# One-core transformer block: four-bank exponentials, gelu straight from PSUM, more tiles turned by transfers, and a new timetable

## The chip, the cores and the metric

The kernel runs on one core of a Trainium2 chip. The metric is the device time of one execution in microseconds (us); smaller is better. The engines are named as in the profile: PE (TensorE, matmuls), PEld (its weight loads), DVE (VectorE), ACT (ScalarE), POOL (GpSimd) and SP (SyncE, which here only issues transfers). PSUM, into which PE writes, has eight banks of 512 fp32 columns.

## What is computed

A pre-layernorm transformer block on x of 2048 rows and 576 columns. The attention has 32 heads of 18 columns and works in four segments of 512 rows: causal softmax attention inside a segment, mixed by a learned gate with a linear-attention memory of the segments before. Then a feed-forward net (FFN) of 4608 columns with gelu. Both have a residual sum.

```python
for s in range(N):                      # N = 4 segments
    logits = einsum('bhqd,bhkd->bhqk', qs, ks) * scale + mask
    a_dot = einsum('bhqk,bhkd->bhqd', softmax(logits), vs)
    pq = phi(qs)                        # phi(t) = t + 1 if t > 0 else exp(t)
    a_mem = einsum('bhld,bhde->bhle', pq, M) / (einsum('bhld,bhd->bhl', pq, z)[..., None] + 1e-06)
    outs.append(g * a_mem + (1.0 - g) * a_dot)
    M = M + einsum('bhld,bhle->bhde', phi(ks), vs)
    z = z + einsum('bhld->bhd', phi(ks))
h = x + concat(outs) @ wo               # q, k, v from layernorm(x)
out = h + gelu(layernorm(h) @ w1 + b1) @ w2 + b2
```

## The kernel before

**Stages.** For each segment s: X (load x, layernorm, turn the tile so that columns lie on partitions), P (projections to q, k, v), A (attention), M (update of the memory), B (output projection, residual sum `h`, second layernorm, turning of the normalised tile into `x2T`), C (first FFN matmul F1, bias and gelu into `hT`), D (second FFN matmul F2, residual sum, output). A tile is 128 rows; a segment has four. In segment 0, stage C runs in two halves: C00 takes tiles 0 and 1, C01 tiles 2 and 3.

**What sets the order.** Each operation is added to a graph with the engines that it may run on. The table `TIMETABLE` (line 26), written into the file, gives each operation a rank and an engine (letter p, a, d, g or s); `Graph.schedule` (line 435) sorts all operations by rank, which fixes the order on every engine, and picks PSUM banks and buffers as it goes. So all engines run fixed sequences, and a late result holds up all that stands behind its reader on the same engine. All transfers but one go down SP's queue in that order; an issue that has to wait for data holds up the issues behind it.

**Tilings of PE.** A matmul uses the full array (128 rows), or half of the rows (two matmuls side by side), a quarter of the rows (scores of 32-row heads, lines 1094 and 1254), or a quarter of the columns (attention values and memory, lines 1125, 1279 and 1228). A projection has two forms, chosen by the order: if its two operations P and R stand side by side they are fused, mostly with full-height matmuls (line 906, with two of half height at an end, line 876); otherwise P and R run as half-height matmuls (line 876, 10 and 8 of them), the halves of the rows change PSUM banks between them, and R waits for a small memset (the mark, line 882) on DVE or POOL.

**Turning tiles.** There are two ways. `transposes` (line 823) uses PE: five (or four) transposes against the identity into a PSUM bank (line 829), then a copy by DVE or ACT into SBUF (lines 710, 706). `flip` (line 696) issues a transposing transfer from SP. In stage X, the pairs of tiles listed in `PE_X` (line 1504) use PE: all of segment 0 and tiles 0 and 1 of segment 1. In stage B of segment 0, tiles 0 and 1 use PE (two calls for each, since the FFN reads the columns in two shifted arrangements, columns 0 to 639 and 64 to 575), and tiles 2 and 3, listed in `DMA_FLIP_0`, use two transfers each.

**Exponentials.** A step of attention writes scores for four heads into two pairs of banks. `exp_of` (line 1045) reads each pair with an ACT instruction of its own (line 1048, 1024 columns), into half of the tile `pt`.

**FFN activation.** For segments 0 to 2, bias is added while a bank is moved from PSUM to `hT` on ACT (lines 1404, 1437) or DVE (lines 1406, 1439); later a few large ACT instructions run gelu in place over a batch of such tiles (lines 1411, 1445), since changing between exp and gelu loads an ACT table. In segment 3, gelu is taken straight from PSUM (line 1396).

**Residual sum in stage B.** The output projection lies in two banks; two DVE instructions of 288 columns add x (line 1331). Then come the statistics (lines 784, 785), the root on POOL (lines 799, 800), normalising (line 815) and a repeat of 64 columns (tail, line 1336).

## Time and profile before

| | |
|---|---|
| median of 3 runs | 440.61 us (440.54 to 441.11) |
| the profiled execution | 440.71 us |
| its span, first to last instruction | 439.0 us |
| granted TensorE clock | 1.000 |
| scores, exp, masks: ACT exponentials (line 1048) | 160, 1022 ns mean |
| first FFN matmuls (lines 1391, 1428) | 972 and 648 |
| second FFN matmuls (line 1480) | 1188 |
| DMA traffic | 72.05 MB, mean 164 GB/s |

The span in 40 slices of 11 us, busy tenths for each engine:

```profile
PE   8989999999999999999999999999999999999997
DVE  6999999988888777887988867585865102000021
ACT  6997978999798798768799977754596002646000
POOL 6888664647546574632522543234222010011010
DMA  7898489899889933965476638406244660650020
```

How to read a profile here: "busy" is the time in which an engine runs instructions; a row `L906 PE MATMUL bank<-hT,xreg ... x242 | 33.3, 287` is line 906, what it writes and reads, how often, total busy us and mean ns of one; what follows the second bar is idle time of the engine just before these, and what ended it. A matmul's own duration (287 ns) overlaps its neighbours, so the time that one occupies is read from the starts of neighbours or from a long group. `SPq` is SP's queue of issues; "landing" is the time from issue until the data is there. The tile names `hT`, `w_lo` and `xreg` are shared: the projection weights lie in `hT`'s space, and `xreg` holds both the turned x tiles and `x2T`.

### The profile page before, as it was taken

To read this page: it belongs to the slowest core of one execution; us is meant where nothing else is said; L and a number is where in the kernel's file an instruction comes from. 1 tells how busy PE (TensorE), PEld (TensorE's weight loads), DVE (VectorE), ACT (ScalarE), POOL (GpSimd) and SP (SyncE) were. 2 spreads that over 40 slices of the span, in tenths; PEclk is the share of its full clock that TensorE was granted. 3 is DMA by queue.
4 is the path that set the end of the run, shared out by engine and by line. 5 is a ranking of instruction groups with operands and counts; after the bars stand their busy time and mean duration, and the time that the engine had idled before them with its cause. 6 is when DMAs were issued, how large, how long until landed. Compare 5 with 4: busy or idle time off the path is not lost.

```text
span 439.0 us, 12146 instructions
## 1 busy us (share of the span) xinstructions
PE 431.3 (98%) x5080; PEld 276.8 (63%) x5080; DVE 285.9 (65%) x622; ACT 298.3 (68%) x328; POOL 175.6 (40%) x332
## 2 busy tenths in 40 slices
PE   8989999999999999999999999999999999999997
PEld 4766677775576676664445766644557775446776
DVE  6999999988888777887988867585865102000021
ACT  6997978999798798768799977754596002646000
POOL 6888664647546574632522543234222010011010
DMA  7898489899889933965476638406244660650020
GB/s 229 192 258 261 138 247 262 198 243 240 187 254 311 327 96 130 194 131 149 159 209 189 136 96 191 119 0 203 83 135 156 165 186 16 198 168 0 1 89 20
DMA packets 78422, 72.05 MB, mean 164 GB/s; under 512 B 57888, under 2 KB 65824, under 8 KB 78368
## 3 DMA queue, kind: packets, MB, share of 16 engines
q1 hardware_dynamic: 78224, 71.20, 59.5%
q8 instruction: 39, 0.64, 0.6%
q14 instruction: 15, 0.12, 0.1%
q10 hardware_dynamic: 144, 0.09, 0.1%
HBM read 42.30 MB, written 15.34 MB: 131 GB/s over the span
## 4 chain that ended last, share of the span: by engine, by line
PE 88%; DVE 7%; DMA 3%; issue 1%; SPq 1%; ACT 0%; DVEq 0%
PE bank L1480 33%; PE bank L1391 24%; PE bank L876 7%; PE bank L1428 7%; PE bank L906 6%; PE bank L1254 4%; PE bank L1279 3%; DMA w1g<-in_B_w_dram 2%; DMA hT<-in_A_w_dram 1%; PE bank L923 1%; DVE qk_pad L710 1%; PE bank L1094 1%; PE bank L1225 1%; DVE pt L1266 1%; PE bank L1125 1%
## 5 line engine op out<-in xcount | busy, mean ns | idle before, releaser
L1048 ACT ACTIVATE pt<-bank 128x1024 bf16<-128x1024 f32 x160 | 155.0, 1022 | 37.2 <-PE bank L1254 21.0
L1480 PEld LDWEIGHTS <-hT 128*128 128x128 bf16 x1188 | 111.7, 98 | 33.0 <-issue 5.8
L1391 PE MATMUL bank<-xreg,w1g 64*128 64x512 bf16 x972 | 108.3, 376 | 0.0
L1391 PEld LDWEIGHTS <-w1g 64*128 64x128 bf16 x972 | 46.6, 94 | 56.4 <-issue 3.4
L1480 PE MATMUL bank<-w,hT 128*128 128x288 bf16 (+2 forms) x594 | 77.5, 283 | 0.0
L1480 PE MATMUL bank<-w_lo,hT 128*128 128x288 bf16 (+2 forms) x594 | 77.2, 283 | 0.0
L1493 DVE TENSOR_TENSOR ot<-bank,hc 128x288 bf16<-128x288 f32 (+2 forms) x33 | 14.1, 443 | 91.7 <-PE bank L1480 90.0
L1268 POOL TENSOR_SCALAR_AFFINE_SELECT pt<-pt 128x512 bf16<-128x512 bf16 x56 | 38.3, 695 | 50.5 <-ACT pt L1048 48.4
L1396 ACT ACTIVATE hT<-bank,b_col 128x512 bf16<-128x512 f32 x36 | 22.3, 689 | 46.1 <-PE bank L1391 46.0
L1466 POOL TENSOR_TENSOR hc<-hc,b_bc 128x576 f32<-128x576 f32 x8 | 10.2, 1274 | 84.0 <-DMA hc<-hd 83.5
L1406 DVE TENSOR_SCALAR hT<-bank,b_col 128x512 bf16<-128x512 f32 x44 | 31.9, 739 | 17.0 <-PE bank L1391 16.0
L1428 PE MATMUL bank<-xreg,w1g 64*128 64x256 bf16 x648 | 38.5, 269 | 0.5 <-DVE qk_pad L710 0.3
L1428 PEld LDWEIGHTS <-w1g 64*128 64x128 bf16 x648 | 31.4, 94 | 6.7 <-issue 3.4
L906 PE MATMUL bank<-hT,xreg 128*128 128x288 bf16 x242 | 33.3, 287 | 0.0
L1411 ACT ACTIVATE hT<-hT 128x8192 bf16<-128x8192 bf16 (+2 forms) x6 | 31.8, 5321 | 0.4 <-DVE hT L1406 0.4
L906 PEld LDWEIGHTS <-xreg 128*128 128x128 bf16 x242 | 22.3, 98 | 7.4 <-issue 0.6
L1266 DVE TENSOR_TENSOR pt<-pt,tri 128x512 bf16<-128x512 bf16 x40 | 21.6, 557 | 8.1 <-ACT pt L1048 8.1
L876 PE MATMUL bank<-hT,xreg 64*128 64x288 bf16 x310 | 25.4, 285 | 1.2 <-DVE mark_dve L882 1.0
L1404 ACT ACTIVATE hT<-bank,b_col 128x512 bf16<-128x512 f32 x28 | 17.8, 686 | 12.3 <-PE bank L1391 11.9
L1439 DVE TENSOR_TENSOR hT<-bank,b_col 128x512 bf16<-128x512 f32 x33 | 21.7, 681 | 4.7 <-PE bank L1428 4.5
L1254 PE MATMUL bank<-qk 32*128 32x512 bf16 (+3 forms) x384 | 23.8, 301 | 0.0
L876 PEld LDWEIGHTS <-xreg 64*128 64x128 bf16 x310 | 14.5, 94 | 11.1 <-issue 5.9
(123 smaller groups left out, 564.0 us busy)
## 6 DMA issues: line engine op xcount, KB each, us to landing
w1g<-in_B_w_dram SPq DMA_DIRECT2D x41, 576.0 KB, 4.6
qkd<-qk_pad SPq DMA_DIRECT2D x12, 512.0 KB, 4.4
hd<-h SPq DMA_DIRECT2D x16, 288.0 KB, 2.7
hc<-hd SPq DMA_DIRECT2D x16, 288.0 KB, 3.7
w_lo<-in_B_w_dram SPq DMA_DIRECT2D x3, 864.0 KB, 5.4
w<-in_B_w_dram SPq DMA_DIRECT2D x3, 864.0 KB, 9.1
xb<-in_A_x_dram SPq DMA_DIRECT2D x16, 144.0 KB, 4.1
out_dram<-ot SPq DMA_DIRECT2D x15, 144.0 KB, 2.2
```

The costliest lines, as they stand in the source:

```text
L876: return nc.tensor.matmul(out=half(hf), lhsT=xTb.t[r, k, ts], rhs=wt[r, hf, k, :], start=start, stop=stop, skip_group_check=True)
L906: nc.tensor.matmul(out=half(hf), lhsT=xTb.t[:, k, ts], rhs=wt[:, hf, k, :], start=(k == 0 and b.form != "first"), stop=(k == n - 1 and b.f ...
L1048: ops.append(add(prio, {"act": 1.04}, lambda e, j=j: nc.scalar.activation(out=pt.t[:, 2 * j:2 * j + 2, :], in_=st[j].t[:], func=ACT.Exp, s ...
L1254: nc.tensor.matmul(out=st[i // 2].t[:, i % 2, off:off + n_], lhsT=qk[rows, 1, kt * P:(kt + 1) * P], rhs=qk[rows, 0, kt * P:L], start=True, ...
L1266: nc.vector.tensor_tensor(out=blk, in0=blk, in1=tri[:].unsqueeze(1).to_broadcast([P, 4, P]), op=ALU.mult)
L1268: nc.gpsimd.affine_select(out=blk, in_=blk, pattern=[[0, 4], [1, P]], compare_op=ALU.is_ge, fill=0.0, base=0, channel_multiplier=-1)
L1391: nc.tensor.matmul(out=cc[w].t[:], lhsT=w1.t[rows, k, q, :], rhs=x2T[s].t[rows, k, :], start=(k == 0), stop=(k == ND - 1))
L1396: ready_f[f + w] = [add(pf - 12, {"act": 0.68}, lambda e, f=f, w=w, cc=cc: nc.scalar.activation(out=hT[:, :, f + w, :], in_=cc[w].t[:].rea ...
L1406: nc.vector.tensor_scalar(out=dst, in0=src, scalar1=b, scalar2=None, op0=ALU.add)
L1411: ge = add(2.9, {"act": 0.42 * (f1 - f0) + 0.2}, lambda e, f0=f0, f1=f1: nc.scalar.activation(out=hT[:, :, f0:f1, :], in_=hT[:, :, f0:f1, ...
L1428: nc.tensor.matmul(out=cc[w].t[:, q * 2 * P:(q + 1) * 2 * P], lhsT=w1.t[rows, k, q, :], rhs=x2T[s].t[rows, k, ts], start=(k == 0), stop=(k ...
L1480: nc.tensor.matmul(out=c.t[:, 0:c1 - c0], lhsT=hT[:, tl // 2, f, (tl % 2) * P:(tl % 2 + 1) * P], rhs=w2_c[ch][:, f - ch * WCH, c0:c1], sta ...
```

## The change

Five edits and a new table:

1. Stage X: `PE_X` loses (1, 0). Tiles 0 and 1 of segment 1 are turned by transfers, as all later x tiles already were.
2. Stage B: all four tiles of segment 0 are turned by two transfers each. The second transfer of tile 0 and both of the other tiles wait for tile 0's first one to have landed.
3. `exp_of`: the second exponential may get the "engine" `whole` (letter w). Then the first instruction reads all four banks (2048 columns), for which it needs four neighbouring banks. The table chooses this 12 times; 136 exponentials stay as they were.
4. Stage C: an eviction may get the "engine" `direct` (letter u): ACT takes gelu with the bias straight from PSUM, and the later in-place gelu leaves that tile out. The table chooses this 20 times.
5. Stage B: the residual sum is one DVE instruction over both banks (576 columns).
6. `TIMETABLE` is new throughout: every engine's order changes.

```diff
-        PE_FLIP_X, PE_X, PE_QK = (0,), ((0, 0), (0, 1), (1, 0)), (0, 1)
+        PE_FLIP_X, PE_X, PE_QK = (0,), ((0, 0), (0, 1)), (0, 1)
...
-                ops.append(add(prio, {"act": 1.04}, lambda e, j=j: nc.scalar.activation(out=pt.t[:, 2 * j:2 * j + 2, :], in_=st[j].t[:], func=ACT.Exp, scale=scale),
+                    if j == 0 and ops[1].eng == "whole":
+                        nc.scalar.activation(out=pt.t[:], in_=banks_all[:, st[0].n:st[0].n + 4, :], func=ACT.Exp, scale=scale)
+                    else:
+                        nc.scalar.activation(out=pt.t[:, 2 * j:2 * j + 2, :], in_=st[j].t[:], func=ACT.Exp, scale=scale)
...
-                for hf, c in enumerate(cc):
-                    cs = slice(hf * HALF, (hf + 1) * HALF)
-                    prev = add(p0 - 0.3, {"dve": 0.45}, lambda e, cs=cs, h=h, c=c, xb=xb: nc.vector.tensor_tensor(
-                        out=h.t[:, cs], in0=c.t[:, 0:HALF], in1=xb.t[:, cs], op=ALU.add), [a, ld, prev], h if hf == 0 else None,
+                    nc.vector.tensor_tensor(out=h.t[:].rearrange("p (f d) -> p f d", f=2), in0=banks_all[:, lo:hi + 1:hi - lo, 0:HALF],
+                                            in1=xb.t[:].rearrange("p (f d) -> p f d", f=2), op=ALU.add)
...
-                if s == 0 and tl in DMA_FLIP_0:
...
-                elif s in PE_FLIP_X:
-                    even = transposes(p0, xn2, [ap], lambda tl=tl: x2T[s].t[:, 0:KT, tl * P:(tl + 1) * P],
...
+                if s == 0:
+                    fl = []
+                    for k0, k1, c0, c1, z in ((0, KT, 0, XW, 275e3), (KT, ND, 64, D, 260e3)):
+                        own = tl == 0 and k0 == 0
+                        fl.append(flip(p0, lambda tl=tl, k0=k0, k1=k1: x2T[0].t[:, k0:k1, tl * P:(tl + 1) * P], lambda xn2=xn2, c0=c0, c1=c1: xn2.t[:, c0:c1], z,
+                                       [ap] + (x2_ok[0][0][:1] if tl else fl[:1]), acq=x2T[0] if own else None, use=[xn2] + ([] if own else [x2T[0]]), cost=1.3))
                     x2_ok[0].append(fl)
...
-                                if e == "act":
-                                    nc.scalar.activation(out=dst, in_=src, func=ACT.Identity, bias=b)
+                                if e in ("act", "direct"):
+                                    nc.scalar.activation(out=dst, in_=src, func=ACT.Identity if e == "act" else ACT.Gelu_apprx_tanh, bias=b)
```

How the compiled orders differ in number (before, after):

| | before | after |
|---|---|---|
| PE: transposes of tiles against the identity | 48 | 20 |
| PE: full-height projection matmuls (line 906) | 292 | 200 |
| PE: half-height projection matmuls (line 876) | 500 | 680 |
| PE: changes of tiling between neighbours | 225 | 214 |
| marks on DVE and POOL (line 882) | 9 and 15 | 14 and 21 |
| ACT: exponentials of 1024 and of 2048 columns | 160 and 0 | 136 and 12 |
| ACT: table loads | 12 | 12 |
| DVE: FFN evictions (lines 1406, 1439) | 77 | 58 |
| causal masks (lines 1106, 1266; 1109, 1268): DVE, POOL | 48, 80 | 42, 86 |
| SP: transposing transfers from SBUF into `xreg` | 14 | 20 |

In SP's new order the transfers of the FFN tiles 0 and 1 follow each other with only stores of q and k among them, ahead of the first FFN matmul; the two new x transfers stand among those that turn q and k of segment 0.

More of the change, by code (lines that the diff above doesn't have):

```diff
@@ L18 @@
 ENGINES = ("pe", "act", "dve", "pool", "sp")
-SWITCH = dict(act=1.35, pe=0.095)
+SWITCH = dict(act=1.35, pe=0.1)
 FUSED = 1.225
@@ L456, in schedule @@
         for op in order:
-            e = op.eng
-            assert e in op.cost and all(a in done for a in op.after + [op.behind] if a is not None), (op.tag, op.name)
+            for f, part in sorted(((f, a) for a, fs in op.parts if a.eng != "direct" for f in fs), key=lambda u: u[0]):
+                if op.runs and op.runs[-1][1] == f:
+                    op.runs[-1][1] = f + 1
+                else:
+                    op.runs.append([f, f + 1])
+            if op.parts:
+                later = [a for a, _ in op.parts if a.eng == "direct"]
+                op.after = [a for a in op.after if a not in later]
+                op.cost = {"act": sum(0.2 + op.each * (b - a) for a, b in op.runs)}
+                op.table = "gelu" if op.runs else None
+        for op in order:
+            e = ON.get(op.eng, op.eng)
+            assert op.eng in op.cost and all(a in done for a in op.after + [op.behind] if a is not None), (op.tag, op.name)
             done.add(op)
+            if op.eng == "whole":
+                op.start, op.end = op.head.start, op.head.end
+                self.release(op, op.end + 0.07)
+                continue
             if op.fence is not None and op.fence.fused:
```

95 lines of the change are left out of this document (51 added, 44 removed), and 635 rows, old and new, of the table TIMETABLE.

## The prediction

> **What bounds the kernel now.** I read the shares first, then the windows, then the chain of waits, then the rows of the stretch that the change touches. The first lines of the page:
>
> ```profile
> span 439.0 us, 12146 instructions
> PE 431.3 (98%) x5080; PEld 276.8 (63%) x5080; DVE 285.9 (65%) x622; ACT 298.3 (68%) x328; POOL 175.6 (40%) x332
> ```
>
> TensorE (PE) is busy for 98% of the span, and it runs its instructions in a fixed order, so the time is its work plus its waits. The windows (engines in the order PE, weight loads, DVE, ACT, POOL; then granted clock and DMA share) tell where the waits are:
>
> ```profile
> 0.00:20.00 20.00, 18.25 (x178) 11.71 (x178) 16.00 (x45) 15.33 (x28) 14.47 (x41) 1.00 0.77 219
> 20.00:40.00 20.00, 18.48 (x334) 12.64 (x330) 18.76 (x46) 18.24 (x22) 16.12 (x36) 1.00 1.04 242
> 40.00:60.00 20.00, 19.71 (x299) 13.75 (x292) 19.37 (x45) 16.78 (x22) 14.68 (x34) 1.00 0.65 200
> ...
> 100.00:120.00 20.00, 19.00 (x264) 11.50 (x264) 17.44 (x34) 17.45 (x23) 13.13 (x21) 1.00 0.91 211
> ...
> 420.00:439.00 19.00, 16.38 (x169) 13.86 (x167) 2.75 (x6) 0.00 (x0) 1.28 (x1) 1.00 0.21 63
> ```
>
> Up to 60 us PE waits 3.6 us, while DVE is busy for 54 of 60: there the short steps on DVE, and the transfers, set the pace together with PE. Between 100 and 120 us PE waits 1.0 us, at the end 2.6 us (the last output leaving), and nearly nothing elsewhere. But "busy" is not yet "at its peak". The long undisturbed stretches of the chain of waits (start, us, what) give the peak, and four short neighbours of the PE timeline give the price of a change of tiling:
>
> ```profile
> 86.40 7.82 PE bank L876 x126
> ...
> 330.44 35.38 PE bank L1480 x288
> 365.83 35.07 PE bank L1391 x324
> ```
>
> ```profile
> 63.68 0.40 PE L1094 MATMUL bank<-w_lo,qk 32*128 32x256 bf16 x8
> 64.01 2.14 PE L1428 MATMUL bank<-xreg,w1g 64*128 64x256 bf16 x36
> 66.08 0.40 PE L1094 MATMUL bank<-w_lo,qk 32*128 32x256 bf16 x8
> ```
>
> A full-height matmul of 288 columns takes 35.38/288 = 0.123 us; a half-height (64-row) one of 512 columns 35.07/324 = 0.108 us, since two run side by side; a half-height one of 288 columns 7.82/126 = 0.062 us. The group of 36 half-height ones of 256 columns occupies 66.08 - 64.01 = 2.07 us, where 36 x 0.054 = 1.95: each change between full, 64-row, 32-row and column tiling costs about 0.1 us. The Trainium skill ("Perfetto Trace Analysis", Identifying the Most-Contended Engine) says that matmul busy share is a poor measure, and weight-load share a good one; by it, 63% would leave much room, and the change could be hidden. The rows decide: laying all 5080 matmuls end to end at the rates above, with 225 changes of tiling, gives 423.2 us of 439.0. So 96% of the span is real PE work, and only 15.8 us are waits, 2.6 of them at the end and some 4 before the first projections are under way.
>
> **The change part by part.** The whole timetable is new, so I count the compiled orders rather than the diff.
>
> *PE work.* Gone are 28 transposes: 10 for x tiles 0 and 1 of segment 1, 18 for the FFN tiles 0 and 1 of segment 0. 18 transposes and their successor stand here:
>
> ```profile
> 49.80 1.20 PE L829 MATMUL bank<-ident,xn 128*128 128x128 bf16 x18
> 50.97 1.14 PE L906 MATMUL bank<-hT,xreg 128*128 128x288 bf16 x8
> ```
>
> 1.17/18 = 0.065 us each, 28 of them 1.8 us. Further, the new order splits more of the projections into two half-height phases: 92 full matmuls go, 180 half-height ones come: 180 x 0.062 - 92 x 0.123 = -0.1 us. The changes of tiling fall from 225 to 214: -1.1 us. Sum on PE: **-3.0 us**. Laid end to end the new order needs 420.4 us (the exact rates round to -2.9).
>
> *Is that work on the path?* After 60 us, yes: PE is full. Of the gain, 1.2 us lie ahead of the first FFN matmul (43.9 us of work ahead of it, before 45.1), 1.7 us behind it. The first part has to be checked against what the transfers bring.
>
> *FFN tiles turned by transfers.* Before, DVE and POOL finish the tile, PE turns it, and DVE and ACT copy it out; the last of these rows releases the first FFN matmul:
>
> ```profile
> 42.05 0.81 DVE L1331 TENSOR_TENSOR h<-bank,xb 128x288 f32<-128x288 f32 x2
> 42.78 0.80 DVE L784 BATCH_NORM_STATS2 ln<-h 128x6 f32<-128x288 f32 x2
> ...
> 47.58 0.54 DVE L815 TENSOR_SCALAR xn<-h,ln 128x576 bf16<-128x576 f32 x1
> ...
> 52.95 0.37 DVE L710 COPY xreg<-bank 128x512 bf16<-128x512 bf16 x1
> ```
>
> ```profile
> 53.38 0.48 PE L1428 MATMUL bank<-xreg,w1g 64*128 64x256 bf16 x5 [0.16 <-DVE xreg L710]
> ```
>
> In the new order tile 0's output projection stands 3.1 us of PE work earlier and DVE takes its steps almost without others between them: projection done at about 30.8 + 7.6 (the waits that PE had collected by then in this trace) = 38.4; sum 0.8, statistics 1.0, the root on POOL 0.9, normalising 0.6, tail 0.2, and some 0.4 of semaphores: 42.3. Then four transfers go down SP's queue:
>
> ```profile
> L697 SPq DMA_TRANSPOSE xreg<-xn x14: 1208/1269/2211, 27.8 to 110.1; - x14
> DMA to landing us min/median/max: 2.6/4.6/6.1
> xreg<-xn SPq DMA_TRANSPOSE x14, 4.1
> ```
>
> (issue in ns, landing over all transfers into xreg, median landing of these 14). The second waits for the first to land: 42.3 + 4.1 = 46.4; the next three issue at 46.4, 47.7 and 48.9, the last lands at 53.0. Behind them in SP's queue stand a store of q and k of segment 1 and the transfer that turns the first x tile of segment 2, which would land at about 55; the projection that reads that tile has 48.2 us of PE work ahead of it, so with these waits it comes at about 57. If this cover of 2 us goes, every later us is PE's loss. PE arrives at 43.9 + 7.6 = 51.5, so it waits 1.5 us and starts the FFN at 53.1, about when it does now. This wait eats the 1.2 us gained ahead of it; what is left is 53.1 - 53.4 - 1.7 = **-2.0 us**. With a landing L the start is 44.8 + 2L: 50.0 (no wait) with the least landing of the row, 57.0 with the largest. I take 4.1, the median of exactly this kind.
>
> The Trainium skill ("VectorE: DVE Perf Modes", The three transpose paths and Rules for kernel authors) advises TensorE for a 128x128 transpose where PSUM will do, at 390 ns against 1309 ns by DMA: a rule against this change. By its prices 28 transposes would free 10.9 us of PE (an estimate from that page) and every transfer would come 0.9 us later. The rows differ: 0.065 us each in a run of 18, so 1.8 us, against 4.1 us to land; the sum goes by them.
>
> *x tiles of segment 1.* Their two transfers stand in SP's queue between those that turn q and k of segment 0; the neighbours issue now at these times:
>
> ```profile
> 13.82 3.18 SPq L697 DMA_TRANSPOSE qk<-qk_pad  x2
> 17.10 2.67 SPq L697 DMA_TRANSPOSE w_lo<-qk_pad  x2
> ```
>
> Put among them, the later of the two issues at about 20 and lands at 24.1; the projection that reads them has 19.8 us of PE work ahead and comes, with the 4.2 us of waits collected by then, at 24.0. With the largest landing it is 2.0 us late, with the least it is early: 0 to +2.0, and I take 0.
>
> *Relief of DVE before 54 us.* The rows of the PSUM copies and of the sum of attention output and x:
>
> ```profile
> L710 DVE COPY xreg<-bank 128x640 bf16<-128x640 bf16 (+1 forms) x5 | 2.3, 461 | 0.0
> L1331 DVE TENSOR_TENSOR h<-bank,xb 128x288 f32<-128x288 f32 x32 | 12.9, 441 | 0.7 <-PE bank L876 0.4 <-issue 0.2
> L1466 DVE TENSOR_TENSOR hc<-hc,b_bc 128x576 f32<-128x576 f32 x8 | 6.4, 801 | 2.6 <-DMA hc<-hd 2.6
> ```
>
> All five copies go, two others come over from ACT: net 3 x 0.46 = 1.4 us off DVE. Summing every DVE instruction ahead of the first FFN matmul at the mean of its group gives 3.3 us less than now (six PSUM evictions fewer, four masks more). The bounds are 0 and -3.3; I take -0.5, as DVE is only one of several releasers here. The sum of attention output and x becomes one instruction of 576 columns: 0.80 (the row of that width) against 0.81 (the pair at 42.05): 0.
>
> *Exponentials over four banks.* 12 pairs become 12 single ones; a pair takes 2 x 1.02 us at most:
>
> ```profile
> L1048 ACT ACTIVATE pt<-bank 128x1024 bf16<-128x1024 f32 x160 | 155.0, 1022 | 37.2 <-PE bank L1254 21.0
> L1396 ACT ACTIVATE hT<-bank,b_col 128x512 bf16<-128x512 f32 x36 | 22.3, 689 | 46.1 <-PE bank L1391 46.0
> L1404 ACT ACTIVATE hT<-bank,b_col 128x512 bf16<-128x512 f32 x28 | 17.8, 686 | 12.3 <-PE bank L1391 11.9
> L1406 DVE TENSOR_SCALAR hT<-bank,b_col 128x512 bf16<-128x512 f32 x44 | 31.9, 739 | 17.0 <-PE bank L1391 16.0
> ```
>
> From 512 to 1024 columns is 0.33 us more, so 2048 come to about 1.7: ACT gains 0.3 each, but the first two banks come free 0.7 later. ACT has idle time, PE does not see it: 0, bounded by 0 and +0.7 x 12 where every bank were missed at once. *Gelu from PSUM*: 20 evictions become gelu at the same price as now (0.689 against 0.686); DVE evicts 19 tiles fewer (19 x 0.74 = 14 us off DVE, where it idles anyway). ACT's table loads stay 12. No gain.
>
> *Marks.* A split projection waits for a small DVE or POOL instruction between its halves. There are 35 instead of 24, and 5 instead of 1 have only one score step (0.3 us) to cover it:
>
> ```profile
> PE bank L876 <- DVE mark_dve L882: 1.0, 1, 1.0
> ```
>
> 24 marks cost one visible wait of 1.0 us. Bounds -1.0 (it goes) and +3 (four short covers at 0.75, the length of a DVE eviction); I take +0.1.
>
> **Sum**: -2.0 - 0.5 + 0.1 = -2.4 us. The profiled execution took 440.71 (1.7 us outside its span), so 438.3; the median of the runs is 0.1 lower: **438.2 us**.
>
> **The rivals.**
> - *All of it lands* (436.3): DVE's relief is 2.4 us instead of 0.5, nearer its bound, and moves the FFN's start with it. For: DVE at 19 of 20 us between 40 and 60. Against: the wait for the first landing remains, and PE work precedes it.
> - *Nothing is left* (440.6): the new order meets other waits of 2.4 us, at marks and at banks. For: 35 marks. Against: behind 60 us PE finds its data in time.
> - *Slower by late transfers* (442.6): the four transfers land at the largest value of the row, 6.1 us, as DMA is at 1.04 of its share between 20 and 40 us. Then the FFN starts at 57.0, 3.6 us later: 3.6 - 1.7 = +1.9. It decides from a landing of 5.6 us on (start at 56.0: loss of 2.6 - 1.7 = 0.9). Against: share 0.65 between 40 and 60, median 4.1. The skill's rule on transposes, above, points to this case.
> - *Slower by the four-bank exponentials* (442.4): six of the twelve make PE wait 0.7 each for their banks, 438.2 + 4.2; it decides from five on (441.7). Against: ACT waits for PE 21 us at these instructions, not PE for ACT.
>
> **How the numbers follow.** Chances: forecast 0.52 (437.2 to 439.4), all of it 0.14, nothing left 0.12, late transfers 0.15, banks 0.07 (together 1). A measurement can tell about 0.2% (0.9 us) from no change. Faster: 0.52 + 0.14 = 0.66, and a little of "nothing left" 0.01; the same 0.11; slower 0.15 + 0.07 = 0.22. The range 436.0 to 441.4 holds the forecast, the first two rivals and the milder third of the late transfers.
>
> **What would show it.** 28 transposes fewer on PE, and not over 2 us of PE waits behind 60 us beside the end; the first FFN matmul at 52.5 to 53.5 us, released by a DMA into xreg; the FFN of segment 3 beginning 2 to 2.5 us before 365.8. A start of the first FFN matmul beyond 56 us, waits of PE for ACT at the scores, or several for marks would make it wrong.

## The result, and the profile after

| | before | changed |
|---|---|---|
| median of the runs taken side by side (us) | 440.81 (440.54 to 441.11, 5 runs) | 446.13 (445.07 to 446.89, 5 runs) |
| ratio, 95% interval | | 1.0113, 1.0096 to 1.0129 |
| profiled execution (us), its span | 440.71, 439.0 | 446.89, 445.2 |

The prediction was 438.2 us, faster; the changed kernel is 5.3 us slower. The profiled execution is the slowest of the five, 0.8 us above the median. In the new kernel line 894 is the half-height projection (876 before), 1423 and 1456 the first FFN matmul (1391, 1428), 1503 the second (1480), 1121 and 1152 scores and values of segment 0 (1094, 1125), 802 the statistics (784), 728 the copies out of PSUM (710), and 1359 the merged residual sum. The page:

```profile
span 445.2 us, 12245 instructions
...
PE 430.5 (97%) x5143; PEld 276.7 (62%) x5143; DVE 276.1 (62%) x595; ACT 301.2 (68%) x347; POOL 176.1 (40%) x331
```

TensorE's work did not grow: by the count of the prediction it is 2.9 us less, laid end to end. So its waits grew, by 9 us. The windows (columns as in the prediction) show one part of them:

```profile
0.00:20.00 20.00, 17.77 (x172) 11.62 (x173) 13.86 (x39) 14.62 (x23) 10.29 (x30) 1.00 0.84 204
20.00:40.00 20.00, 16.63 (x343) 10.49 (x340) 18.80 (x45) 16.71 (x23) 15.09 (x28) 1.00 1.07 224
40.00:60.00 20.00, 18.77 (x284) 12.39 (x286) 17.51 (x42) 18.10 (x23) 13.13 (x31) 1.00 0.88 249
```

TensorE is idle for 2.2 + 3.4 + 1.2 = 6.8 us in the first 60, where it was 3.6 before. What it waited for behind 56 us shows the other part (the two largest rows of its waits; columns: us in total, times, longest):

```profile
PE bank L1423 <- DVE h L1359: 2.3, 3, 0.9
PE bank L894 <- DVE h L1359: 1.8, 2, 0.9
```

Both lie on VectorE's merged residual sum; the kernel before had no row for it. To follow the two parts I use TensorE's **lag**: the start of an instruction less the work ahead of it, laid end to end as in the prediction (changed kernel, first FFN matmul: 56.35 - 43.86 = 12.5 us).

| start (us) and lag (us) | before | changed | changed with sums in halves |
|---|---|---|---|
| first key projection of segment 1 | 25.1, 4.6 | 27.3, 7.5 | 27.3, 7.6 |
| first FFN matmul | 53.4, 8.3 | 56.4, 12.5 | 56.5, 12.7 |
| second FFN product of segment 2 | 330.4, 12.9 | 353.9, 21.6 | 349.8, 17.5 |

(The second FFN product of segment 2 stands elsewhere in the two orders, so only its lag compares.) Ahead of the first FFN matmul the change lost 4.2 us, behind it another 4.5; less 2.9 of work that is 5.8 of the 6.2 us by which the span of the profiled execution grew. With the sums in halves (the first experiment below) the lag at the first FFN matmul stays (12.7), and behind it 4.8 us are added, about the 4.6 of before.

The places that the prediction named, in the timelines of TensorE and of SP's queue and in the chain of waits of the changed kernel:

```profile
56.35 1.91 PE L1456 MATMUL bank<-xreg,w1g 64*128 64x256 bf16 x32
```

```profile
46.23 1.22 SPq L715 DMA_TRANSPOSE xreg<-xn  x1
...
48.60 5.30 SPq L715 DMA_TRANSPOSE xreg<-xn  x3
```

```profile
371.68 35.07 PE bank L1423 x324
```

The first FFN matmul starts 3 us later than before and has no wait of its own in its row; the four transfers of the FFN tiles are issued from 46.2 to 53.9, and the last one lands at 55.1, 1.2 us ahead of it. The FFN of segment 3 begins at 371.7, not 2 us before 365.8.

### The profile page after: what moved, and what is told of

The parts are those of the page before. It is cut to its first block, busy times and chain, and to the rows that moved or that the text cites. A ratio compares the mean times of both kernels' runs of the same rounds, so it can differ in the third digit from the quotient of the medians.

```text
span 445.2 us, 12245 instructions
## 1 busy us (share of the span) xinstructions
PE 430.5 (97%) x5143; PEld 276.7 (62%) x5143; DVE 276.1 (62%) x595; ACT 301.2 (68%) x347; POOL 176.1 (40%) x331
## 5 line engine op out<-in xcount | busy, mean ns | idle before, releaser
L1072 ACT ACTIVATE pt<-bank 128x1024 bf16<-128x1024 f32 x136 | 132.1, 1023 | 31.6 <-PE bank L1281 21.2
L1428 ACT ACTIVATE hT<-bank,b_col 128x512 bf16<-128x512 f32 x36 | 22.4, 686 | 45.9 <-PE bank L1423 45.8
L1389 ACT ACTIVATE hT<-hT 128x512 bf16<-128x512 bf16 (+10 forms) x20 | 40.6, 2077 | 0.2
L894 PE MATMUL bank<-hT,xreg 64*128 64x288 bf16 x456 | 35.2, 284 | 2.0 <-DVE qk_pad L728 0.8
L1436 ACT ACTIVATE hT<-bank,b_col 128x512 bf16<-128x512 f32 x43 | 27.1, 688 | 14.7 <-PE bank L1423 10.6
L894 PEld LDWEIGHTS <-xreg 64*128 64x128 bf16 x456 | 21.1, 94 | 13.2 <-issue 5.3
L1438 DVE TENSOR_SCALAR hT<-bank,b_col 128x512 bf16<-128x512 f32 x29 | 20.9, 744 | 13.0 <-PE bank L1423 13.0
L1070 ACT ACTIVATE pt<-bank 128x2048 bf16<-128x2048 f32 x12 | 22.5, 1879 | 6.9 <-PE bank L1281 5.0
L924 PE MATMUL bank<-hT,xreg 128*128 128x288 bf16 x168 | 23.6, 287 | 0.2 <-DMA xreg<-xn 0.2
L817 POOL TENSOR_SCALAR ln<-ln 128x1 f32<-128x1 f32 x32 | 8.9, 277 | 37.3 <-DVE ln L803 36.9
L1261 DVE STREAM_TRANSPOSE t<-bank 128x512 f32<-128x512 f32 x24 | 16.8, 700 | 8.0 <-PE bank L1252 4.0
```

The costliest lines, as they stand in the source:

```text
L894: return nc.tensor.matmul(out=half(hf), lhsT=xTb.t[r, k, ts], rhs=wt[r, hf, k, :], start=start, stop=stop, skip_group_check=True)
L924: nc.tensor.matmul(out=half(hf), lhsT=xTb.t[:, k, ts], rhs=wt[:, hf, k, :], start=(k == 0 and b.form != "first"), stop=(k == n - 1 and b.f ...
L1070: nc.scalar.activation(out=pt.t[:], in_=banks_all[:, st[0].n:st[0].n + 4, :], func=ACT.Exp, scale=scale)
L1072: nc.scalar.activation(out=pt.t[:, 2 * j:2 * j + 2, :], in_=st[j].t[:], func=ACT.Exp, scale=scale)
L1389: nc.scalar.activation(out=at, in_=at, func=ACT.Gelu_apprx_tanh)
L1428: ready_f[f + w] = [add(pf - 12, {"act": 0.68}, lambda e, f=f, w=w, cc=cc: nc.scalar.activation(out=hT[:, :, f + w, :], in_=cc[w].t[:].rea ...
```

## The experiments

All times are medians; each was taken beside the kernel before, at 440.7 to 441.3 us. A new timetable can make the planner choose other PSUM banks. Most kernels below therefore hold its choice by a table, and their line numbers are higher by some 60 to 80 (L1190 can then be line 1121, L963 line 894, L797 line 728); where banks are chosen anew, the text says so. `qk_pad` and `v_aug` are the tiles into which q, k and v are copied out of PSUM.

### The merged residual sum

Here are its rows by source line in the changed kernel (duration in ns; then what its engine waited for and who waited for it: us, times), and two of the places:

```profile
L1359 DVE TENSOR_TENSOR h<-bank,xb x16: 695/757/758, 41.6 to 339.5; 128x576 f32<-128x576 f32 x16
...
  PE bank L894: 7.2, 4
```

```profile
158.62 0.76 DVE L1359 TENSOR_TENSOR h<-bank,xb 128x576 f32<-128x576 f32 x1 [0.45 <-issue]
161.85 0.76 DVE L1359 TENSOR_TENSOR h<-bank,xb 128x576 f32<-128x576 f32 x1 [1.88 <-PE bank L894]
```

```profile
159.43 2.38 PE L894 MATMUL bank<-wt_o,oT 64*128 64x288 bf16 x36 [0.91 <-DVE h L1359]
162.66 0.54 PE L894 MATMUL bank<-wt_o,oT 64*128 64x288 bf16 x6 [0.85 <-DVE h L1359]
```

By the planner's choice the sum at 158.62 reads banks 0 and 4, and the projection at the head of the group that waits for it at 159.43 writes banks 3 and 7. It needs neither bank 0 nor bank 4, but 3 lies between them. **Theory**: the strided access `banks_all[:, lo:hi + 1:hi - lo, ...]` counts as touching every bank from the lower to the upper one. **Rival**: the sum is just long, and frees its own banks 0.35 us later than the first half did.

```diff
-                    nc.vector.tensor_tensor(out=h.t[:].rearrange("p (f d) -> p f d", f=2), in0=banks_all[:, lo:hi + 1:hi - lo, 0:HALF],
-                                            in1=xb.t[:].rearrange("p (f d) -> p f d", f=2), op=ALU.add)
+                    for f, n in enumerate((lo, hi)):
+                        cs = slice(f * HALF, (f + 1) * HALF)
+                        nc.vector.tensor_tensor(out=h.t[:, cs], in0=banks_all[:, n, 0:HALF], in1=xb.t[:, cs], op=ALU.add)
```

> The changed kernel with the sum of the residual emitted as two half-width instructions, each on one bank, in the place of the one that reads two banks through a strided access; order, engines and banks as in the changed kernel. Theory (the one access counts as touching every bank from its lower to its upper one, so TensorE's writes to banks in between wait for it): the five waits of 0.9 to 1.1 us at 159, 163, 322, 325 and 335 us go, no bank L894 or L1423 waits for DVE h any more, and the time falls by 4 to 5.5 us to 441 to 442 us, with the lag of TensorE behind its own work at the first FFN matmul (12.5 us) unchanged. Rival (the sum is long, 0.76 us, and frees its two banks only at its end, 0.35 us later than the first half did): TensorE waits only for the sum's own banks, the saving is at most 5 times 0.35 us = 1.8 us and the time is 444.5 us or more.

Measured: 442.04 us, ratio to before 1.0029 (1.0016 to 1.0042). That is 4.1 us less than the changed kernel, as much as the two rows of waits for the sum had (2.3 + 1.8), at the edge of the theory and far from the rival's 444.5. Order and banks are those of the changed kernel. The largest row of TensorE's waits is now

```profile
PE bank L847 <- DVE xn L831: 1.2, 2, 0.8
```

(a start-up wait), no row names the sum, and the lag at the first FFN matmul is unchanged (12.7).

The same edit the other way round, on the kernel before:

```diff
-                for hf, c in enumerate(cc):
-                    cs = slice(hf * HALF, (hf + 1) * HALF)
...
+                    nc.vector.tensor_tensor(out=h.t[:].rearrange("p (f d) -> p f d", f=2), in0=banks_all[:, lo:hi + 1:hi - lo, 0:HALF],
+                                            in1=xb.t[:].rearrange("p (f d) -> p f d", f=2), op=ALU.add)
```

> The kernel before with one edit: its 16 pairs of half-width residual sums become 16 sums over two banks each (in the third stage of the segments these are banks 5 and 7, 2 and 3, 6 and 0, 4 and 6, then 1 and 3, 2 and 6, 4 and 5, 7 and 0, then 1 and 2, 0 and 3, 7 and 6, 4 and 5). Theory (every bank between counts): slower by 1.5 to 6 us, to 442.3 to 447 us, with waits of TensorE for DVE h of 0.8 us or more where a sum over far banks is followed by a projection into a bank between. Rival (nothing but the two banks is held, and the merged sum's 0.03 us saving on each of 16 counts): 440.3 to 441.5 us, no TensorE wait for h above 0.4 us.

Measured: 445.68 us, 1.011 (1.0096 to 1.0123): +4.8 us. (The planner chose banks anew here; the next kernel has the same banks and the same order.) Its timelines (VectorE, then TensorE) show both directions of the wait:

```profile
245.67 0.76 DVE L1332 TENSOR_TENSOR h<-bank,xb 128x576 f32<-128x576 f32 x1 [1.47 <-remote]
...
326.24 0.76 DVE L1332 TENSOR_TENSOR h<-bank,xb 128x576 f32<-128x576 f32 x1 [1.22 <-PE bank L1392]
```

```profile
246.48 0.38 PE L1225 MATMUL bank<-e,MZ_blk 128*128 128x512 bf16 x1 [1.06 <-DVE h L1332]
...
327.05 2.12 PE L1392 MATMUL bank<-xreg,w1g 64*128 64x512 bf16 x18 [0.91 <-DVE h L1332]
```

The sum at 245.67 reads banks 2 and 6. Ahead of it in the compiled order stands a product into bank 3, which lies between, and the sum waits 1.47 us for it (the trace has both products' weight loads, at 245.1, but lost the record of this matmul, so it names no releaser); the product that then waits 1.06 us for the sum writes bank 2, one of the sum's own. The sum at 326.24 reads banks 0 and 3, whose projection had ended before 321.7; it waited 1.22 us for FFN matmuls into banks 1 and 2, and the next FFN matmuls, into bank 0, then waited 0.91 us for it. So a sum over distant banks first runs late, because of writes in between, and then holds TensorE up; in the changed kernel, at 159.43, it also holds up a write into a bank in between. All of these waits stand as semaphores in the compiled programs: the order is one that the program is given, and whether the chip would need it no run shows.

Last, merged sums only where the banks are neighbours (the edit against the kernel just above):

```diff
+                    if hi - lo > 1:
+                        for f, n in enumerate((lo, hi)):
...
+                        return
                     nc.vector.tensor_tensor(out=h.t[:].rearrange("p (f d) -> p f d", f=2), in0=banks_all[:, lo:hi + 1:hi - lo, 0:HALF],
```

> The kernel before with the merged residual sum only where its two banks are neighbours (9 of the 16 sums), the other 7 in halves. Theory (only the banks between are held in vain, and neighbours have none): 440.3 to 441.2 us, as the kernel before, and no wait of TensorE for a merged sum above 0.4 us. Rival (a merged sum costs by its length and its later end, whatever its banks): 9 of 16 of the 4.8 us that all 16 cost, 443 us or more.

Measured: 441.12 us beside 441.34, 0.9983 (0.9954 to 1.0013): nine merged sums at no cost that the interval shows (up to 0.6 us stays possible; the rival asked for 443 or more), and no row of its waits names a merged sum. It differs from the kernel above by the seven distant sums alone, so the cost is in the banks passed over. This is **shown**.

### Four-bank exponentials

In the timetable each `w` (the second half taken in by the first) becomes an ordinary exponential again:

```diff
-    "A00exp": "a81 w87 a103 a124",
+    "A00exp": "a81 a87 a103 a124",
```

> The changed kernel with its 12 four-bank exponentials undone, each as two two-bank exponentials in the same place of ScalarE's order. Theory (the loss is in the sums and in VectorE's order of the first 60 us, and ScalarE has cover): within 0.7 us of the changed kernel's 446.1 us, ScalarE's busy time higher by 12 x (2 x 1.09 - 1.8) = 4 to 5 us. Rival (a four-bank exponential holds four banks until its end and the scores behind it come late): faster by 1 to 3 us.

Measured: 448.11 us, 1.0165 (1.0149 to 1.018). Neither theory: ScalarE was busy only 0.8 us longer (302.0 for 301.2), the lag at the first FFN matmul fell by 1.0, but TensorE's waits for the merged sums grew from 4.1 to 5.2 us. The planner chose banks anew here, and the sums got others (one pair is 2 and 7 where it was 2 and 5), so this time does not tell what the exponentials are worth. I held the banks and undid both:

> The changed kernel with both the half-width residual sums (442.0 us) and the 12 four-bank exponentials undone; banks and order otherwise held. Theory (a four-bank exponential keeps four banks until its end and delays the first 27 us: with the exponentials alone undone the lag of TensorE behind its work was 6.5 us at the first key projection of segment 1 in place of 7.5, and 11.5 in place of 12.5 at the first FFN matmul, and only the residual sums' waits, which grew there, hid it): 440.5 to 441.5 us. Rival (four-bank exponentials are worth 2 us to the whole kernel, which is what undoing them alone cost, 448.1 against 446.1): 443.5 to 444.5 us.

Measured: 441.59 us, 1.0014 (1.0001 to 1.0027), against 442.04 with halves alone, 1.0029 (1.0016 to 1.0042). The intervals overlap: four-bank exponentials cost 0.5 us or nothing, and are not worth the 2 us of the rival. That they cost anything is not shown. With the banks held, the first FFN matmul starts only 0.2 us earlier (56.31 for 56.52), so the 1.0 us of lag that went in the run before was not theirs alone.

### What the transfers are worth

Both parts put back on TensorE, each in the changed kernel with sums in halves (442.04 us), banks held:

```diff
-        PE_FLIP_X, PE_X, PE_QK = (0,), ((0, 0), (0, 1)), (0, 1)
+        PE_FLIP_X, PE_X, PE_QK = (0,), ((0, 0), (0, 1), (1, 0)), (0, 1)
...
+    "X1TX": "p 137.3 140.3",
+    "X1copy": "d 137.6 140.6",
```

> The changed kernel with half-width residual sums (442.0 us) and the first two x tiles of segment 1 turned by TensorE again, each in five transposes and a copy on VectorE ahead of the projections of segment 1; banks otherwise held, FFN tiles still by transfers. Theory (turning these tiles by transfers needs their normalised tiles early, and the statistics and normalising that are put ahead for it in VectorE's order hold TensorE up): this edit leaves them early and only drops the transfers, so it shows the transfers' own share: with 0.65 us of transposes and two copies more, 442.3 to 443.5 us, the waits for qk_pad and v_aug unchanged. Rival (the transfers themselves are late for the first projections of segment 1, or crowd out the loads of weights and FFN tiles in the first 60 us): the lag at P1Pv[1], 10.3 us, falls by 1 us or more and the time is 439.5 to 441.3 us.

Measured: 443.54 us, 1.0066 (1.0048 to 1.0084), 1.5 us more. That is the theory's side, at its upper end: the early waits stay without these transfers, and the transposes add their own (the first one waits 1.46 us behind VectorE's copies):

```profile
24.26 0.44 PE L919 MATMUL bank<-ident,xn 128*128 128x128 bf16 x5 [1.46 <-DVE qk_pad L800]
```

```diff
+                if s == 0 and tl not in DMA_FLIP_0:
+                    even = transposes(p0, xn2, [ap], lambda tl=tl: x2T[s].t[:, 0:KT, tl * P:(tl + 1) * P],
...
+    "B00T": "p 328.1 335.1",
+    "B01T": "p 328.2 335.2",
```

> The changed kernel with half-width residual sums (442.0 us) and the first two FFN tiles of segment 0 turned by TensorE again: 18 transposes and four copies ahead of the first FFN matmul in the place of four transfers; banks otherwise held. Theory (the transfers were in time: TensorE arrived at 56.3 us when they had landed and did not wait): TensorE has 18 x 0.065 = 1.2 us more work, up to 0.4 us of changes of tiling and a wait of up to 0.5 us for the last copy, nothing comes back: 443 to 444.2 us. Rival (their four turning transfers and the flips and loads behind them hold up the x and qk tiles that TensorE waits for between 40 and 60 us): 440 to 441.5 us, with the waits for qk_pad and v_aug between 44 and 56 us, 0.9 us, gone.

Measured: 442.82 us, 1.0045 (1.0028 to 1.0062). That is 0.8 us more, somewhat under the theory's range and far from the rival; the intervals still overlap. The first FFN matmul starts at 57.3, 0.8 us later, and waits 0.6 us for the copy. Turning the FFN tiles by transfers is not what costs.

The x transfers alone, in the order of the kernel before:

```diff
-    "X1TX": "p 142 152",
-    "X1apart": "d 106 122",
-    "X1copy": "d 143 153",
-    "X1apply": "d 169 164",
-    "X1flip": "s 229 208",
+    "X1apply": "d 106 122 169 164",
+    "X1flip": "s 118.2 130.5 229 208",
```

> The kernel before with one part of the change alone: the first two x tiles of segment 1 turned by transfers from SBUF, normalised at the same places of VectorE's order and issued as soon as they are, the second waiting for the first to land; ten transposes and two copies go. Theory (two transfers one behind the other land too late for the first projection of segment 1, which the kernel before starts at 25.1 us): it starts at 26.5 to 28 us, released by the transfer, and the time is 441.5 to 443 us. Rival (the transfers land in time, or VectorE's relief pays for it): 439.5 to 440.7 us.

Measured: 443.82 us, 1.0066 (1.0044 to 1.0089), +2.9 us: slower, as the theory says, but not by its way. The projection came in time. In the kernel before, the load of the next x tile went out at 20.77; then SP's queue, VectorE and TensorE in this kernel:

```profile
20.77 0.38 SPq L690 DMA_DIRECT2D x<-in_A_x_dram  x1
```

```profile
18.43 3.39 SPq L764 DMA_TRANSPOSE xreg<-xn  x2
21.87 1.30 SPq L764 DMA_TRANSPOSE w_lo<-qk_pad  x1
23.22 0.57 SPq L757 DMA_DIRECT2D x<-in_A_x_dram  x1
```

```profile
27.71 0.82 DVE L851 BATCH_NORM_STATS2 ln<-x 128x6 f32<-128x288 bf16 x2 [2.15 <-DMA x<-in_A_x_dram]
...
29.92 0.75 DVE L777 CAST qk_pad<-bank 128x576 bf16<-128x576 f32 x1
```

```profile
30.73 0.61 PE L1161 MATMUL bank<-qk 32*128 32x128 bf16 x14 [2.42 <-DVE qk_pad L777]
```

The two transfers occupy SP's queue for 3.4 us, so the load of the next x tile is issued only at 23.2, 2.4 us later than before. VectorE's statistics wait 2.15 us for it, the copy into `qk_pad` stands behind them, and TensorE waits 2.42 us for that copy. The victim of the transfers here is whoever is queued behind them, two engines further on.

### VectorE's order ahead of the first FFN matmul

In the changed kernel the statistics of x tiles 2 and 3 of segment 1 stand early in VectorE's order, and VectorE stopped there for a load (1.28 us at 18.8). First they were moved:

```diff
-    "X1apply": "d 85 99 182 129",
-    "X1rstd": "g 78 98 100 119",
-    "X1stats": "d 74 75 97 110",
+    "X1apply": "d 85 99 182 163.6",
+    "X1rstd": "g 78 98 128.6 160.6",
+    "X1stats": "d 74 75 128.5 160.5",
```

> The changed kernel with the statistics of the third and fourth x tiles of segment 1 moved later in VectorE's order, behind the copies and powers of keys that segment 0's first stages need (the third behind the copy into v_aug and the power of keys that now follow it, the fourth and its normalising just ahead of its transfers), and their inverse deviations on GpSimd with them; banks and all else as in the changed kernel. Theory (these statistics stop VectorE's queue at 18.8 us, 1.3 us for the x tile's load, while TensorE waits for qk_pad and v_aug behind them): TensorE's lag at the first FFN matmul falls from 12.5 to 10.5 to 11.5 us, the time by 1 to 2 us to 444 to 445 us. Rival (FFN tiles' transfers land at 56.3 us whatever PE does, and they set the FFN's start): the lag at P1Pv[1], 36 us, falls by 1 us or more and the first FFN matmul stays at 56.2 to 56.5 us; time within 0.5 us of 446.1 us.

Measured: 448.39 us, 1.0167 (1.0153 to 1.0181), against 446.13: slower, lag at the first FFN matmul 13.4. Neither theory. TensorE's waits for VectorE between 20 and 26 us did shrink, but it then met another:

```profile
PE bank L963 <- DMA xreg<-xn: 2.0, 1, 2.0
```

Next, with halves, the same with x tiles 0 and 1 on TensorE, so that this transfer is out of the way (the timetable of the run above and of the x tiles, together):

> The changed kernel with half-width residual sums and the first two x tiles of segment 1 on TensorE (443.5 us), and the statistics of the third and fourth moved later in VectorE's order as well, behind the work of segment 0. Theory (with the two tiles by transfers, the statistics ahead cost TensorE 1.5 us of waits for VectorE between 20 and 26 us, and moving them alone showed nothing because TensorE then waited 2.0 us for the transfer): with neither, the waits for qk_pad and xreg between 20 and 30 us, 2.2 us in that kernel, fall below 0.8 us and the time is 441.8 to 442.5 us. Rival (VectorE is late there from its sheer work and order, not from these statistics): 443 to 444 us.

Measured: 444.55 us, 1.0092 (1.0066 to 1.0118): the theory fails, TensorE waits 2.1 us for `qk_pad` at the next scores. And with the second tile's transfer moved ahead in SP's queue:

```diff
-    "X1flip": "s 86 125 210 168",
-    "P01flip": "s 135 151 92 130",
-    "wodma": "s 158 96",
+    "X1flip": "s 86 99.1 210 168",
+    "P01flip": "s 135 151 99.2 130",
+    "wodma": "s 158 99.3",
```

> The changed kernel with half-width residual sums (442.0 us), the statistics of the third and fourth x tiles of segment 1 later in VectorE's order, and the transfer that turns the second x tile issued right behind that of the first, ahead of a flip of segment 0's powers (w_lo) and a load of weights. Theory (the order on VectorE and the order on the queue of transfers each hold TensorE until 27.3 us at the first key projection of segment 1): that projection starts by 26 us, lag 6.3 us or less in place of 7.6, and the time is 440.3 to 441.2 us, if w_lo is not late in turn. Rival (the queue has no room: what is put ahead makes w_lo's flip late by the same 1.3 us and the scores with the earlier keys wait for that): 441.6 to 443 us, with a new wait for a transfer between 28 and 40 us.

Measured: 442.89 us, 1.0046 (1.0031 to 1.0061). The first key projection of segment 1 now starts at 25.5 without a wait for a transfer, as the theory has it, but the time is the rival's: the scores then wait 2.1 us for the copy into `qk_pad`, behind the moved statistics. So the copy went first:

```diff
-    "X1apply": "d 85 99 182 163.6",
-    "X1stats": "d 74 75 128.5 160.5",
-    "gates": "a126 d161",
+    "X1apply": "d 85 99 182 167.5",
+    "X1stats": "d 74 75 128.5 166.5",
+    "gates": "a126 d166.4",
```

> The changed kernel with half-width residual sums, the statistics of the third x tile of segment 1 later, the second x tile's transfer ahead (442.9 us so far), and now the fourth tile's statistics and three short steps on the gates moved behind the copy into qk_pad for which TensorE waited 2.1 us at 31.3 us. Theory (of the 3.8 us lost ahead of the first FFN matmul, most comes from the places that VectorE's and the queue's orders give to what segment 1 needs, ahead of what segment 0 needs at once; no part of the change needs these places): the 2.1 us go, the granted clock stays at 1.0 between 32 and 36 us, TensorE's lag at the first FFN matmul is 10 to 11 us in place of 12.7, and the time 439.6 to 440.8 us. Rival (each wait taken away is replaced by the next one, as with the other moves): lag 12 us or more, 441.5 us or more.

Measured: 444.29 us, 1.0072 (1.0047 to 1.0098): the rival. The copy itself now waits for a transfer, and TensorE loses 2.98 us at the next step (VectorE, TensorE):

```profile
29.05 0.76 DVE L797 CAST qk_pad<-bank 128x576 bf16<-128x576 f32 x1 [1.41 <-DMA w_lo<-qk_pad]
```

```profile
34.56 1.81 PE L1105 MATMUL bank<-v_aug,fk_pad 128*128 128x76 bf16 x32 [2.98 <-DVE t L1235]
```

Finally, with halves and x tiles 0 and 1 on TensorE, the statistics of x tiles 2 and 3 were left out altogether (constants stand in for them):

```diff
+                if skip:
+                    nc.vector.memset(sm.t[:, 12:14], 1.0)
+                    return
```

> Work left out: the kernel with half-width residual sums and the first two x tiles of segment 1 on TensorE (443.5 us), without the statistics of the third and fourth tile of segment 1 (constants stand in for them, so these tiles are not normalised by their own mean and deviation). VectorE has 3.7 us less to do before 25 us and does not wait for these tiles' loads there. Theory (VectorE's work and waits put ahead of segment 0's copies are what holds TensorE between 20 and 33 us): the waits for qk_pad and xreg, 3.1 us in that kernel, fall by 2 us or more and the time to 440.5 to 441.7 us. Rival (VectorE is fed late there by others, and its statistics only fill the gaps): 442.8 to 443.6 us.

Measured: 443.77 us, 1.0051 (1.0035 to 1.0068), against 443.54 with them: the rival. With 3.7 us less to do VectorE itself stood idle, waiting 1.79 us for TensorE at 20.9, and TensorE waited for VectorE at 23.7, 26.1 and 31.7. So the load of these statistics is not the cause; here each of the two engines stops for the other.

### The two orders joined

Operations that the kernel before ranks below 372, about where its first FFN matmuls begin, keep its ranks and engines; all others follow in the order of the changed kernel. Sums are in halves, and x and FFN tiles on TensorE as before. One row of the new timetable (92 and 113 are the ranks of the kernel before):

```diff
-    "A00st0": "p 69 101",
...
+    "A00st0": "p92 p113",
```

> A kernel of two orders: every operation that the kernel before has ahead of its first FFN matmul (53 us) keeps that kernel's order and engine, and all that follows takes the changed kernel's order and engines, gelu from PSUM and the later four-bank exponentials among them; x and FFN tiles are turned as before, residual sums are half-width. TensorE has the same columns to multiply as before and 218 changes of tiling in place of 225. Theory (all that is lost beside the sums is lost ahead of the first FFN matmul, by the changed kernel's order and transfers there): the lag at the first FFN matmul is the 8.3 us of before, it grows no more from there than before's (4.6 us), and the time is 439.8 to 440.8 us. Rival (the changed order loses behind the first FFN matmul too, which the sums hid): 441.5 us or more.

Measured: 442.58 us, 1.0035 (1.0022 to 1.0048). The first FFN matmul starts at 53.18 with 45.06 us of work ahead: lag 8.1, as before. But two waits, 2.9 us together, stand behind the joint, at 104.6 and 57.4 us:

```profile
PE bank L957 <- ACT qk_pad L787: 1.6, 1, 1.6
PE bank L1184 <- DVE t L1229: 1.3, 1, 1.3
```

With the joint 16 operations later (388 in place of 372):

> The kernel of two orders again, joined 16 operations later, behind the first FFN matmul, where TensorE waited 1.3 us (57 us) and 1.6 us (105 us) at the joint before. Theory (the changed order loses nothing behind the first FFN matmul, and only the joint's waits made 442.6 us of it): those two waits fall below 1.5 us together and the time is 440 to 441.2 us. Rival (the later part of the changed order loses by itself): 442 us or more with other waits behind 110 us.

Measured: 440.92 us, 0.9999 (0.9987 to 1.0011). Both waits are gone; one of 1.3 us stands at the new joint (62.2 us), and behind it no wait is over 0.4 (the profiled execution, of 442.19 us, lost another 1.4 us at 10.2 us to a load of weights):

```profile
PE bank L957 <- ACT pt L1135: 1.3, 1, 1.3
...
PE bank L1315 <- DVE v_aug L791: 0.4, 1, 0.4
```

This is the theory: the rest of the new order costs nothing that can be measured, and with the lags above (4.8 us behind the first FFN matmul with sums in halves, 4.6 before) it follows that **what is lost beside the sums is lost ahead of the first FFN matmul**, by the transfers and the order that the change has there.

### A version that beats both

The kernel before has one visible wait on its path, the 1.0 us for marks at 109.66 that the prediction quotes. VectorE was in the middle of a power of keys of 1.16 us there:

```diff
-    "P2fk": "d 484 539 600 654",
+    "P2fk": "d 484 539 600 658.5",
```

> The kernel before with one instruction of VectorE moved: the power of keys at 108.4 us (1.16 us long) goes behind the two marks that TensorE waits 1.0 us for at 109.66 us. Theory (this one wait of TensorE is on the path, and nothing else is late for it): 439.7 to 440.2 us, faster than the kernel before by 0.6 to 1.0 us and faster than the changed kernel by 6. Rival (what needs the power of keys, or the copies behind it, is late in turn): 440.5 to 441.2 us.

Measured: 440.04 us (12 runs), 0.9975 (0.9964 to 0.9986): 0.9 us faster than before, and 6 us faster than the changed kernel. The 36 matmuls around the marks now run through:

```profile
107.38 2.49 PE L946 MATMUL bank<-hT,xreg 64*128 64x288 bf16 x36
```

## Why the prediction was wrong

1. *"The sum of attention output and x becomes one instruction ...: 0"* is the step that failed most. Its duration was right (0.757 us; 0.80 assumed), but only duration was priced. Which banks it holds, and what is written between them, was not asked. Where the banks were not neighbours, the program ordered it against every write into the banks between. It cost **4.1 us** (halves), 4.8 on the kernel before.
2. *"PE arrives at 43.9 + 7.6 = 51.5"* failed by 4.9 us: the 7.6 us of waits were carried over from the old order, and the new one collects 12.5. So the gain ahead of the first FFN matmul (1.2 of work) and the start at 53.1 fell. What the sums leave of the miss is 442.0 - 438.2 = **3.8 us**, and the lags and the joined orders place it in the stretch ahead of that matmul. Which instruction is to blame stays open: four-bank exponentials account for 0.5 at most; x transfers, FFN transfers and the early statistics, taken back one at a time, gave nothing back. Taken back together with the order, they did.
3. *FFN tiles*: the chain of transfers was priced well in kind. But the tiles were ready 3.9 us later than the 42.3 assumed (first transfer at 46.2), so the last one landed at 55.1 and not at 53.0; it met a TensorE that was later still (56.35). A TensorE in time would have waited for it. Their worth, as run, is the 0.8 us that going back costs, not 2.0 ("-2.0 us" failed). The rival of late transfers (442.6) did not happen: the first took 4.3 us to land and the last 2.5, not 6.1, and no wait for them shows.
4. *x tiles, "0 to +2.0"*: +2.9 in the order of before, outside the range. The landing was priced, the queue behind it was not, nor the drop of the clock after the long wait (below).
5. *Relief of DVE*, -0.5: VectorE's busy time ahead of 60 us fell from 54.1 to 50.2 us, somewhat over the bound of 3.3, and the lag grew all the same; leaving out statistics of 3.7 us brought nothing either. That speaks for VectorE's order, and against its load, as what holds TensorE in this stretch; which place in the order it is, no run shows.
6. *Exponentials*, 0: right within what was measured. One takes 1.88 us (1.7 estimated) where the pair takes 2 x 1.02. *Gelu from PSUM*, 0: no wait speaks against it; it was not run alone.
7. *Marks*: the 1.0 us went, as the lower bound had it; two marks between 20 and 26 us made TensorE wait 0.4 and 0.3 us.
8. *PE work*, -3.0: stands by count. "Not over 2 us of PE waits behind 60 us" was broken by the sums alone.

None of the four rivals named the mechanism; the one called "nothing is left" (other waits, at marks and at banks) came nearest, with 2.4 us for what became 8.7.

## What to carry to other kernels

Before one access over several PSUM banks takes the place of several accesses, list the banks from its first to its last and who writes them meanwhile; choose neighbours, or stay with one access per bank. Where two engines and a queue of transfers are all nearly full, a wait that is taken away mostly uncovers the next, so the waits of the old order are no forecast for a new one; a new order can be judged by joining it to the old one at a point where both have done the same work. A moved transfer costs what is queued behind it, which may be a load for another engine.

## What the runs showed of the hardware

The granted clock of TensorE fell to one half for some microseconds around the end of a single wait of over 2 us. The windows of the kernels with x transfers in the old order (wait of 2.42 us until 30.7), with statistics later and x tiles on TensorE (2.12 until 32.7), and with the transfer ahead (2.12 until 31.3); the third column from the right is the clock:

```profile
30.00:32.00 2.00, 1.27 (x18) 0.73 (x18) 2.00 (x4) 0.66 (x1) 1.36 (x3) 0.60 1.04 373
32.00:34.00 2.00, 2.00 (x19) 1.39 (x17) 2.00 (x5) 1.52 (x3) 1.28 (x3) 0.55 1.42 242
```

```profile
34.00:36.00 2.00, 2.00 (x23) 1.63 (x22) 1.90 (x5) 1.67 (x3) 1.89 (x4) 0.50 0.61 163
```

```profile
32.00:34.00 2.00, 2.00 (x14) 1.38 (x13) 2.00 (x4) 1.70 (x3) 1.89 (x5) 0.50 1.05 224
```

Worked out from such windows, the drop began between 0.3 us before the wait's end (first kernel: 0.60 means 1.6 us at one half ahead of 32.0) and 0.9 us after it, and it lasted 3.4 us in each (first kernel: 1.6 and 1.8 us). In the first kernel it takes 1.27 x 0.40 + 2.00 x 0.45 = 1.4 us of its +2.9, and in the others 1.6 and 1.7, so the times of these kernels hold more than the wait. Not every execution has it: the mean clock over the span is 0.992 to 0.996 in all six of the first kernel, but 0.996 in only two of four in each of the others. After the wait of 2.04 us (statistics moved alone) the clock stayed at 1.00:

```profile
28.00:30.00 2.00, 2.00 (x80) 1.32 (x76) 1.53 (x7) 1.18 (x2) 1.10 (x4) 1.00 1.03 324
```

The Trainium skill ("TensorE: Matmul & The Clock Gate", HAM oscillation — how this bites in real kernels) puts the rule as no idle gaps of TensorE above about 3.4 us. Here waits of 2.1 us, with shorter ones around them, were enough in some executions, and the measured wait is the one to go by here.
